# A three-block kernel on one core: the weights' sign by a Prelu, the masks made on chip, the first two tiles in another order

## The chip, the core and the metric

The kernel runs on one core of a Trainium2 chip. A core has a matrix engine (PE, with its weight loads shown apart as PEld), a vector engine (DVE), an engine for activation functions (ACT), GpSimd (POOL) and a queue (SP) that starts the DMA transfers. Each engine takes its own instructions strictly in their order, and waits where an operand or a buffer is not ready. The metric is the time of one execution on the device, in microseconds.

## The reference

Three blocks follow one another on 3072 rows (4 sequences of 768):

```python
la = log_a[:, :, sl]; cum = np.cumsum(la, axis=-1)          # per chunk
L = np.exp(cum[:, :, :, None] - cum[:, :, None, :]) * causal
M = np.einsum('bhin,bhjn->bhij', Cc, Bc) * L
y = M @ xc + (Cc @ state) * exp(cum)                        # attention with a state that is handed on
state = decay_full * state + sum(Bc x xc * decay_from_j)
...
h = y @ w_in;  g = relu(h)**2;  x2 = g @ w_out              # first block: 256 -> 2048 -> 256
a = x2 @ w1;  b = x2 @ w2                                   # second block: 256 -> 1024
out = ((a * b) @ w3) @ w_out2                               # 1024 -> 1024 -> 256
```

All inputs and the result are float32.

## The kernel before, in words

**Products.** Every float32 operand of a product is split into a high part, rounded to the matrix engine's format, and a low part, which is what is left over. A product is three passes (low by high, high by high, high by low). ACT or POOL rounds the high part (`split`, `part_hi`, `conv_parts`), DVE subtracts (`split_lo`, L141).

**Weights.** They come as 44 pieces of 128 x 512 float64 words: 16 of kind "a" (`w_in` and `w_out` of the first block), 4 "o", 16 "3" and 8 "12". SP loads a piece (512 KB), and the kernel makes float32 of it by bit operations on the words: ACT scales the upper words into a float32 (`conv_words`, L196), and for some pieces the lower words too (`ACT_LOW`, L198); otherwise DVE shifts the lower words (L206). Then DVE joins upper and lower words (L207), and a second DVE instruction puts the sign bit in (L210). `conv_parts` then splits the piece (L228 on POOL or L230 on ACT, then L141). Pairs of "3" pieces are multiplied with the "o" pieces on the matrix engine (`w3_product`, L257), so that w3 and the last weight become one.

**Tiles.** The rows are worked off in 6 tiles of 512. A tile has a phase A of 16 steps (`h_mm`, L819: six products of 512 columns; relu on ACT, L833; square on ACT, L841, or DVE, L843; the split; and, a few steps late, `x2_mm`, L866: six more) and a phase B of 8 steps (`a_mm`, `b_mm`, L819 again, and `out_mm`, L919). `SEQ` puts phase A of the second tile straight behind that of the first. In these two phases the pieces are converted, `RATE` pieces a step. `SQ_DVE` names the steps of these two phases whose square DVE takes.

**Attention.** It goes in chunks of 96 rows. Chunks 0 to 5 (units 0 to 2, two chunks each) are worked in `startup`, ahead of all steps; the later ones are placed in slots of the steps (`attention_plan_1` for the chunks of the second tile, `attention_plan` for the rest). The start needs the decays: log(a) by ACT (L343), products with 0/1 masks (L419, L455), which come by DMA as 128 x 904 numbers, exponentials, and from them `e_first`. For a unit, `unit_e1` (L663, L668, then Exp on ACT, L671) spreads the decays, `unit_pad` (L602) and `unit_bi` (L607) prepare C and B, `unit_g0` (L637) multiplies them, `unit_m0` (L679) multiplies both, `chunk_pre` (L578, POOL) scales x, `chunk_ds` (L717) makes the state that `chunk_hand` (L724) hands to the next chunk, and `chunk_y_mm` (L755) makes the result, which `chunk_out` splits into `xt`, the input of the first step.

**What sets the order.** In `startup` and in phase A of the first tile the order on each engine is that of the code (`in_order`, `held`). Behind that a scheduler of the compiler orders the instructions. DMAs keep the order in which the code issues them.

Of the kernel before, what the change touches and what calls it, by code (L numbers as in the profile page):

```python
# [58 lines left out]
def kernel(  # L59
# [969 lines left out]
    def attention_plan_1():  # L1029
        ph = ("A", 0)  # L1030
        for j, s in enumerate(ASLOT):
            g = FIRST[1] + j
            put(ph, s, chunk_pre, g)
            put(ph, s, chunk_mask, g)
            put(ph, s + 1, chunk_g, g, 0)
            put(ph, s + 1, chunk_g, g, 1)
            put(ph, s + 2, chunk_y, g)
        put(ph, 1, unit_bc, 4, BCPLACE)
        put(ph, 1, conv_load, 2)
        for s in range(2):  # L1040
            put(ph, 1 + s, unit_e1, 3, 2 * s, False)
            put(ph, 1 + s, unit_e1, 3, 2 * s + 1, False)
        put(ph, 4, unit_e, 4)
        put(ph, 7, unit_split, 5)
        put(ph, 10, unit_bc, 5)
# [266 lines left out]
```

## Time and profile before

| | us |
|---|---|
| median of three runs | 560.01 |
| lowest, highest | 557.99, 560.12 |
| the profiled execution | 559.61 |
| its span in the profile | 557.9 |

Some 1.7 us of the profiled execution lie outside the span. The profile has, for each engine, the time in which it was busy; the span in stretches; the chain of work that ended last; and groups of like instructions with their mean duration and the idle time of the engine before them. Matrix products are pipelined: a product of 512 columns is shown with some 390 ns, but six of them follow one another in 1.36 us, so a busy matrix engine is not one at its peak. The last three columns of the windows are the clock granted to the matrix engine (as a share of the full one), the DMA share and GB/s.

### The profile page before, as it was taken

How to read it: one execution, taken by the hardware profiler on the slowest of the kernel's cores; microseconds unless marked ns; L12 is line 12 of the kernel's file. 1: busy time of each engine (PE TensorE's matmuls, PEld its weight loads, DVE VectorE, ACT ScalarE, POOL GpSimd, SP SyncE). 2: the span in 40 equal slices, each digit the busy share in tenths (PEclk: the TensorE clock that was granted, in tenths of full speed). 3: DMA queues.
4: the chain of work that ended last, by engine and by line, in shares of the span. 5: the costliest groups of instructions: out<-in, count | busy, mean ns of one | idle time of the engine just before them, and what ended most of it. 6: DMA issues, size and time to landing. Idle time of an engine off the chain costs nothing.

```text
span 557.9 us, 9140 instructions
## 1 busy us (share of the span) xinstructions
PE 544.0 (98%) x3340; PEld 448.5 (80%) x3340; DVE 367.6 (66%) x665; ACT 284.3 (51%) x543; POOL 88.1 (16%) x136
## 2 busy tenths in 40 slices
PE   7979999999999999999999999999999999999997
PEld 5757777889888888888888888888888888888886
DVE  5689999987989575576576556574566474554431
ACT  6699768877875322354333354342435332444332
POOL 7344750000000221004031004020012010000000
PEclk9889999999999999999999999999999999999999
DMA  8697592143454561067250066120173220100001
GB/s 235 231 307 225 176 374 91 39 152 114 164 173 126 135 160 53 0 156 177 68 133 17 16 156 170 24 79 1 36 168 100 57 70 0 39 0 2 0 1 38
DMA packets 56573, 59.46 MB, mean 107 GB/s; under 512 B 33360, under 2 KB 44624, under 8 KB 56528
## 3 DMA queue, kind: packets, MB, share of 16 engines
q1 hardware_dynamic: 56528, 58.88, 36.8%
q8 instruction: 26, 0.43, 0.3%
q14 instruction: 19, 0.16, 0.1%
HBM read 50.20 MB, written 8.65 MB: 105 GB/s over the span
## 4 chain that ended last, share of the span: by engine, by line
PE 81%; DVE 8%; ACT 4%; DMA 4%; issue 1%; SPq 1%; DVEq 0%; ACTq 0%
PE mm L819 43%; PE acc L866 19%; PE acc L919 10%; PE mm L257 4%; PE acc L928 2%; PE y L755 2%; PE g L618 2%; DVE gp L141 2%; DMA xb<-in_xb_dram 1%; DMA raw<-in_raw_dram 1%; DVE cvs L207 1%; DVE wa L141 1%; SPq L93 1%; DVE cvs L210 1%; DMA u<-in_w_dram 1%
## 5 line engine op out<-in xcount | busy, mean ns | idle before, releaser
L819 PE MATMUL mm<-xt,wa 128*128 128x512 f32 x576 | 148.7, 395 | 3.2 <-DVE wa L141 2.0
L849 ACT CAST gp<-tmp 128x512 fp32r<-128x512 f32 x144 | 89.3, 622 | 119.4 <-DVE tmp L907 64.3
L866 PE MATMUL acc<-gp,wa 128*128 128x512 f32 x576 | 146.4, 392 | 1.3 <-DVE gp L141 0.7
L141 DVE TENSOR_TENSOR gp<-tmp,gp 128x512 fp32r<-128x512 f32 x144 | 103.0, 718 | 62.7 <-ACT gp L849 61.9
L819 PE MATMUL mm<-x,w 128*128 128x512 f32 x576 | 143.4, 392 | 0.0
L819 PEld LDWEIGHTS mm<-xt,wa 128*128 128x128 f32 x576 | 107.4, 190 | 26.8 <-ACT tmp L833 2.4
L866 PEld LDWEIGHTS acc<-gp,wa 128*128 128x128 f32 x576 | 106.4, 188 | 24.5 <-DVE gp L141 1.5
L819 PEld LDWEIGHTS mm<-x,w 128*128 128x128 f32 x576 | 105.9, 188 | 21.7 <-ACT tmp L899 0.2
L833 ACT ACTIVATE tmp<-mm 128x512 f32<-128x512 f32 x96 | 57.3, 597 | 50.9 <-PE mm L819 50.2
L919 PE MATMUL acc<-gp,w3o 128*128 128x512 f32 x240 | 63.7, 391 | 0.0
L843 DVE TENSOR_TENSOR tmp<-tmp 128x512 f32<-128x512 f32 x68 | 46.9, 692 | 24.0 <-ACT tmp L833 23.5
L559 POOL TENSOR_SCALAR_AFFINE_SELECT e<-e 96x768 f32<-96x768 f32 x26 | 25.3, 985 | 236.3 <-DMA e<-e_d 228.9
L907 DVE TENSOR_TENSOR tmp<-tmp,mm 128x512 f32<-128x512 f32 x48 | 33.0, 687 | 42.9 <-PE mm L819 42.4
L919 PEld LDWEIGHTS acc<-gp,w3o 128*128 128x128 f32 x240 | 44.8, 188 | 9.4
L899 ACT COPY tmp<-mm 128x512 f32<-128x512 f32 x48 | 28.2, 587 | 41.0 <-PE mm L819 40.7
L578 POOL TENSOR_TENSOR xb<-xb,dec 96x256 f32<-96x256 f32 x32 | 23.1, 723 | 91.9 <-DMA xb<-in_xb_dram 89.2
L624 DVE TENSOR_TENSOR e<-g,e 128x384 f32<-128x384 f32 x52 | 27.6, 551 | 6.5 <-PE g L618 6.0
L257 PE MATMUL mm<-wo,w 128*128 128x256 f32 x128 | 23.7, 284 | 0.4 <-DVE w L141 0.3
L745 DVE SCALAR_TENSOR_TENSOR xb<-xb,through,y 32x64 f32<-32x64 f32 x72 | 20.3, 282 | 3.1 <-PE y L717 1.3
L257 PEld LDWEIGHTS mm<-wo,w 128*128 128x128 f32 x128 | 20.6, 190 | 2.0 <-DVE w L141 1.0
L618 PEld LDWEIGHTS g<-cb,bt 96*128 96x128 f32 x96 | 16.6, 190 | 3.3
L257 PE MATMUL mm<-wo2l,w 128*128 128x256 f32 x64 | 18.1, 283 | 0.0
(111 smaller groups left out, 476.9 us busy)
## 6 DMA issues: line engine op xcount, KB each, us to landing
u<-in_w_dram SPq DMA_DIRECT2D x24, 512.0 KB, 3.9
ua<-in_w_dram SPq DMA_DIRECT2D x16, 512.0 KB, 7.0
e<-e_d SPq DMA_DIRECT2D x40, 192.0 KB, 5.1
xb<-in_xb_dram SPq DMA_DIRECT2D x32, 192.0 KB, 3.8
bt<-hl_d SPq DMA_DIRECT2D x78, 48.0 KB, 2.1
hl_d<-gp SPq DMA_DIRECT2D x9, 384.0 KB, 2.6
cb<-hl_d SPq DMA_DIRECT2D x66, 48.0 KB, 2.0
out_dram<-gp SPq DMA_DIRECT2D x20, 128.0 KB, 3.0
```

What stands on the lines that cost most here:

```text
L141: return nc.vector.tensor_tensor(out=lo, in0=src, in1=hi.bitcast(F32), op=ALU.subtract)
L257: nc.tensor.matmul(acc[:, :DM], v[:, l, e % 4 * P:(e % 4 + 1) * P], wo2[1 + e // 2][r][:, e % 2 * DM:(e % 2 + 1) * DM], start=(n == 0), st ...
L618: nc.tensor.matmul(ps[:, 2 * pp:2 * pp + 2], w, un["c2"][:, pr, :, j * CH:(j + 1) * CH], start=True, stop=True)
L624: nc.vector.tensor_tensor(out=m, in0=ps, in1=m, op=ALU.mult)
L819: i = nc.tensor.matmul(ps, w[m][:, l, col + k * P:col + (k + 1) * P], rhs[k][:, r, :], start=((l, r, k) == (1, 0, 0)), stop=((l, r, k) == ...
L833: nc.scalar.activation(r, ps, AF.Relu)
L843: nc.vector.tensor_tensor(out=g32, in0=r, in1=r, op=ALU.mult)
L849: nc.scalar.copy(g[:, 0, :], d[k])
L866: i = nc.tensor.matmul(acc["x2", t][e], wa[m][:, l, 256 + e * P:256 + (e + 1) * P], g[:, r, :], start=(m == 0 and n == 0), stop=(m == MF - ...
L899: nc.scalar.copy(s, ps)
L907: nc.vector.tensor_tensor(out=p32, in0=prods[t, m], in1=ps, op=ALU.mult)
L919: nc.tensor.matmul(acc["o"][e].rearrange("p s e -> p (s e)"), w3o[m // 2][:, l, m % 2, e * P:(e + 1) * P], g[:, r, :], start=(m == 0 and n ...
```

## The change

The upper words are scaled by a Prelu whose slope for negative numbers is 2^32 times larger, with the sign turned: a negative word comes out positive, with its exponent 32 higher, and the shift by three that joins the words then moves that bit into the sign. The second DVE instruction goes. The masks are no longer loaded whole: 128 x 136 numbers come, and DVE makes the rest (`masks_made`, `masks_inside`, `masks_halves`) with a memset and subtractions. `a` comes without its padding. Which engine rounds a first-block piece's high part, squares and lower words changes (13 of 16 such pieces on POOL as before, but others; `SQ_DVE` 5 and 8 steps instead of none and 4; 12 of the "3" pieces' lower words on ACT instead of 8), and `RATE` of the second tile's phase A goes from 1.55 to 2.1 pieces a step. `startup` and `attention_plan_1` are written in another order; in `startup`, `unit_m0` is now placed one quarter at a time.

```diff
-AHEAD = 6
-ASLOT = (6, 9, 13, 17, 21)
+AHEAD = 5
 LOW_SCALE, LOW_BIAS = 2.0 ** -29 - 2.0 ** -42, 2.0 ** -12 - 0.5
-ACT_LOW = {"a": (0, 1, 2, 3), "o": (), "3": (1, 3), "12": ()}
+ACT_LOW = {"a": (0, 1, 2, 3), "o": (), "3": (0, 2, 3), "12": ()}
...
-SQ_DVE = {0: (), 1: (3, 4, 5, 6)}
+SQ_DVE = {0: (3, 8, 9, 11, 14), 1: (0, 1, 2, 3, 4, 6, 8, 10)}
...
-RATE = {("A", 0): (1, 0), ("A", 1): (1.55, 3), ("B", 0): (1, 0)}
+RATE = {("A", 0): (1, 0), ("A", 1): (2.1, 3), ("B", 0): (1, 0)}
...
         lo_w, hi_w = stage[i][:, :, 0], stage[i][:, :, 1]
-        keep(nc.scalar.activation(v, hi_w.bitcast(F32), AF.Copy, scale=2.0 ** -112))
+        keep(nc.scalar.activation(v, hi_w.bitcast(F32), AF.Prelu, scale=2.0 ** -112, alpha=-2.0 ** 32))
...
         if not act_low(i):
-            nc.vector.tensor_single_scalar(lo_w, lo_w, 29, op=ALU.logical_shift_right)
+            with held():
+                nc.vector.tensor_single_scalar(lo_w, lo_w, 29, op=ALU.logical_shift_right)
         nc.vector.scalar_tensor_tensor(
             out=v, in0=v, scalar=3, in1=lo_w, op0=ALU.logical_shift_left, op1=ALU.bitwise_or
-        )
-        nc.vector.scalar_tensor_tensor(
-            out=v, in0=hi_w, scalar=0x80000000, in1=v, op0=ALU.bitwise_and, op1=ALU.bitwise_or
         )
...
-        if kind == "a" and j > 2:
+        if kind == "a" and j in (0, 1, 3, 4, 6, 7, 8, 9, 10, 11, 12, 13, 15):
             nc.gpsimd.tensor_copy(w[:, 0, :], v)
...
-    m_rel = new_tmp()
-    m_oth = new_tmp()
+    m_all = wts.tile([P, 780], F32, tag="wo0", name="masks")
+    m_rel, m_cum, m_in, m_aft = m_all[:, :512], m_all[:, 512:648], m_all[:, 648:776], m_all[:, 776:]
...
+        nc.vector.memset(warm, 1.0)
+        nc.vector.memset(m_rel, 0.0)
+        nc.scalar.activation(warm, warm, AF.Ln)
...
-        nc.gpsimd.memset(cb.bitcast(F32), 0.0)
...
+        nc.gpsimd.memset(cb.bitcast(F32), 0.0)
...
-    def decays_load(k):
-        if k == 0:
-            dma(out=la, in_=a)
-        elif k == 1:
-            dma(out=m_rel, in_=masks[:, 0:512])
-        else:
-            c = (slice(256, 392), slice(0, 256))[k - 2]
-            dma(out=m_oth[:, c], in_=masks[:, 512 + c.start:512 + c.stop])
+    def decays_load():
+        dma(out=la[:, :192], in_=a[:, :192])
+        dma(out=m_cum, in_=masks[:, 768:904])
+
+    def masks_made():
+
+        nc.vector.tensor_scalar(
+            out=m_aft, in0=m_cum[:, 31:128:32], scalar1=-1.0, scalar2=1.0, op0=ALU.mult, op1=ALU.add
+        )
+        for b in range(4):
+            nc.vector.tensor_scalar(
+                out=m_rel[:, b * P + 32 * b:b * P + P], in0=m_cum[:, 32 * b:P],
+                scalar1=m_cum[:, 32 * b + 31:32 * b + 32], scalar2=None, op0=ALU.subtract
+            )
+
+    def masks_inside():
+
+        c = m_cum[:, :P].rearrange("p (b i) -> p b i", b=4)
+        nc.vector.tensor_tensor(
+            out=m_in.rearrange("p (b i) -> p b i", b=4), in0=c[:, :, 31:32].to_broadcast([P, 4, 32]), in1=c,
+            op=ALU.subtract
+        )
+
+    def masks_halves():
+        nc.vector.tensor_reduce(
+            out=halves, in_=m_cum[:, P:].rearrange("p (q h) -> p h q", h=2), op=ALU.add, axis=mybir.AxisListType.X
+        )
...
+        put(ph, 0, unit_e1, 3, 1, False)
+        put(ph, 0, unit_e1, 3, 3, False)
+        put(ph, 2, unit_e1, 3, 2, False)
+        put(ph, 2, unit_bc, 4, BCPLACE)
+        put(ph, 3, decays_e_out)
+        put(ph, 3, conv_load, 2)
...
-        decays_load(0)
-        decays_load(1)
-        decays_load(2)
-        decays_load(3)
+        decays_load()
+        chunk_xb(0)
+        picks, rounded = constants()
+        picks(0, nc.vector)
         batch_load(0, 0, 1)
-        batch_load(1, 0, 1)
-        chunk_xb(0)
+        picks(1, nc.gpsimd)
         chunk_xb(1)
         batch_load(0, 1, 3)
+        rounded()
+        decays_ln()
+        batch_load(1, 0, 1)
+        masks_made()
+        masks_inside()
+        masks_halves()
+        chunk_xb(2)
+        decays_e_first()
+        decays_cols()
+        unit_e1(0, 1)
...
```

What the new order does on the engines is shown by three places. The first is the DMA queue at the start (`raw` are B and C of the first sequence, the first `raw` of a pair B, `xb` the chunks' x, `ua` first-block pieces). Before:

```order
L93 DMA tmp<-in_a_dram 128x256
L93 DMA tmp<-in_masks_dram 128x512
L93 DMA tmp<-in_masks_dram 128x136
L93 DMA tmp<-in_masks_dram 128x256
L93 DMA raw_111<-in_raw_dram 128x256
L93 DMA raw_113<-in_raw_dram 128x256
L93 DMA xb<-in_xb_dram 96x512 x2
L93 DMA raw_111<-in_raw_dram 128x2x256
L93 DMA raw_113<-in_raw_dram 128x2x256
L93 DMA xb<-in_xb_dram 96x512 x4
L93 DMA ua_129<-in_w_dram 128x1024
```

Now:

```order
L92 DMA tmp<-in_a_dram 128x192
L92 DMA masks<-in_masks_dram 128x136
L92 DMA xb<-in_xb_dram 96x512
L92 DMA raw_153<-in_raw_dram 128x256
L92 DMA xb<-in_xb_dram 96x512
L92 DMA raw_153<-in_raw_dram 128x2x256
L92 DMA raw_170<-in_raw_dram 128x256
L92 DMA xb<-in_xb_dram 96x512
L92 DMA raw_170<-in_raw_dram 128x2x256
L92 DMA ua_245<-in_w_dram 128x1024
L92 DMA raw<-in_raw_dram 128x2x192
```

The two large mask transfers are gone, and three chunks of x stand ahead of the second C transfer (the second `raw` of the later pair) where two did.

The second is the matrix engine in the start, from the second state product (L717 before, L737 now) to the product of B and C for unit 1 (L637 before, L657 now). Before:

```order
L668 MATMUL mm<-e_first,pick 128x192 x2
L717 MATMUL y<-xb,pb 32x64 x4
L755 MATMUL mm<-e,xb 32x96 x8
L663 MATMUL mm<-nmask,ident 128x384
L668 MATMUL mm<-e_first,pick 128x192 x2
L663 MATMUL mm<-nmask,ident 128x384
L668 MATMUL mm<-e_first,pick 128x192 x2
L637 MATMUL g<-cp,bi 128x192 x8
L717 MATMUL y<-xb,pb 32x64 x4
```

Now:

```order
L737 MATMUL y<-xb,pb 32x64 x4
L683 MATMUL mm<-nmask,ident 128x384
L688 MATMUL mm<-e_first,pick 128x192 x2
L683 MATMUL mm<-nmask,ident 128x384
L688 MATMUL mm<-e_first,pick 128x192 x2
L657 MATMUL g<-cp,bi 128x192 x8
```

The result of chunk 0 (L755) stood ahead of unit 1's B and C product; now it stands behind unit 2's (not shown), and two more decay spreads stand between.

The third is DVE around the first step's weights (`cvs` is the joined piece, `wa_...` its split, `gp<-tmp,gp` the split of a step's square, `hl` that of B and C). Before, from the second piece on:

```order
L207 SCALAR_TENSOR_TENSOR cvs<-cvs,ua_133 128x512
L210 SCALAR_TENSOR_TENSOR cvs<-ua_133,cvs 128x512
L141 TENSOR_TENSOR hl<-raw,hl 128x192 x2
L141 TENSOR_TENSOR wa_579<-cvs,wa_579 128x512
L207 SCALAR_TENSOR_TENSOR cvs<-cvs,ua_135 128x512
L210 SCALAR_TENSOR_TENSOR cvs<-ua_135,cvs 128x512
L207 SCALAR_TENSOR_TENSOR cvs<-cvs,ua_399 128x512
L141 TENSOR_TENSOR gp<-tmp,gp 128x512
L210 SCALAR_TENSOR_TENSOR cvs<-ua_399,cvs 128x512
L207 SCALAR_TENSOR_TENSOR cvs<-cvs,ua_506 128x512
L141 TENSOR_TENSOR wa_599<-cvs,wa_599 128x512
L210 SCALAR_TENSOR_TENSOR cvs<-ua_506,cvs 128x512
```

Now, from the same piece's split on:

```order
L140 TENSOR_TENSOR wa_546<-cvs,wa_546 128x512
L140 TENSOR_TENSOR hl<-raw,hl 128x192 x2
L207 SCALAR_TENSOR_TENSOR cvs<-cvs,ua_375 128x512
L140 TENSOR_TENSOR wa_609<-cvs,wa_609 128x512
L207 SCALAR_TENSOR_TENSOR cvs<-cvs,ua_379 128x512
L140 TENSOR_TENSOR wa_662<-cvs,wa_662 128x512
L207 SCALAR_TENSOR_TENSOR cvs<-cvs,ua_377 128x512
L140 TENSOR_TENSOR gp<-tmp,gp 128x512
L207 SCALAR_TENSOR_TENSOR cvs<-cvs,ua_399 128x512
L140 TENSOR_TENSOR wa_617<-cvs,wa_617 128x512
L140 TENSOR_TENSOR wa_688<-cvs,wa_688 128x512
L140 TENSOR_TENSOR gp<-tmp,gp 128x512
```

Each piece has one instruction ahead of its split where it had two, and the first two pieces are split ahead of the first step's squares.

## Rows read from the trace of the kernel before

**Rows 1.** The page, part 1: busy us, share of span, instructions.
```profile
PE 544.0 (98%) x3340; PEld 448.5 (80%) x3340; DVE 367.6 (66%) x665; ACT 284.3 (51%) x543; POOL 88.1 (16%) x136
```

**Rows 2.** Windows: length, then busy PE, PEld, DVE, ACT, POOL, granted clock, DMA.
```profile
0.00:28.00 28.00, 23.68 (x372) 18.31 (x372) 16.92 (x43) 17.80 (x41) 15.35 (x38) 0.94 0.75 234
28.00:45.00 17.00, 13.53 (x53) 10.18 (x53) 15.58 (x23) 16.56 (x36) 8.86 (x11) 0.90 0.86 263
45.00:91.50 46.50, 44.71 (x300) 35.03 (x301) 45.91 (x81) 35.67 (x73) 22.32 (x27) 1.00 0.76 255
91.50:157.00 65.50, 64.48 (x371) 55.91 (x369) 55.71 (x98) 54.93 (x102) 0.00 (x0) 1.00 0.31 105
157.00:228.00 71.00, 71.00 (x429) 58.37 (x428) 51.84 (x102) 29.90 (x59) 11.18 (x17) 1.00 0.45 122
```

**Rows 3.** Timeline of PE, 28 to 95: start, length, instruction, [idle before].
```profile
28.06 1.65 PE L819 MATMUL mm<-xt,wa 128*128 128x512 f32 x6 [0.87 <-ACT xt L144]
...
91.49 3.56 PE L819 MATMUL mm<-xt,wa 128*128 128x512 f32 x15
```

**Rows 4.** Groups of PE, 28 to 91.5: count, busy us, mean ns, idle before.
```profile
L819 PE MATMUL mm<-xt,wa 128*128 128x512 f32 x100 | 28.0, 419 | 3.0 <-DVE wa L141 2.0 <-ACT xt L144 0.9
L866 PE MATMUL acc<-gp,wa 128*128 128x512 f32 x96 | 25.8, 399 | 0.9 <-ACT gp L849 0.6 <-DVE gp L141 0.3
```

**Rows 5.** Chain of waits: start, length, what (whole span).
```profile
5.03 6.23 DMA raw<-in_raw_dram
...
16.02 1.59 PE g L637 x16
...
239.40 2.27 PE acc L866 x10
...
263.50 1.36 PE mm L819 x6
...
322.06 2.27 PE acc L866 x10
```

**Rows 6.** Groups of DVE, 28 to 91.5.
```profile
L141 DVE TENSOR_TENSOR wa<-cvs,wa 128x512 fp32r<-128x512 f32 x15 | 13.7, 912 | 0.6 <-ACT wa L230 0.6
...
L210 DVE SCALAR_TENSOR_TENSOR cvs<-ua,cvs 128x512 uint32<-128x512 uint32 x15 | 11.5, 766 | 0.1
...
L206 DVE TENSOR_SCALAR uo<-uo 128x512 uint32<-128x512 uint32 x4 | 2.3, 574 | 0.0
...
L206 DVE TENSOR_SCALAR u<-u 128x512 uint32<-128x512 uint32 x4 | 1.7, 424 | 0.0
```

**Rows 7.** Groups of ACT, 28 to 91.5.
```profile
L841 ACT ACTIVATE tmp<-tmp 128x512 f32<-128x512 f32 x16 | 10.1, 632 | 0.3
...
L196 ACT ACTIVATE cvs<-ua 128x512 f32<-128x512 f32 x14 | 9.4, 675 | 0.0
```

**Rows 8.** Groups of ACT, 91.5 to 157.
```profile
L230 ACT CAST w<-cv 128x512 fp32r<-128x512 f32 x18 | 11.0, 620 | 2.3 <-DVE cv L210 2.2
...
L198 ACT ACTIVATE u<-u 128x512 uint32<-128x512 uint32 x8 | 5.4, 677 | 0.0
```

**Rows 9.** Groups of DVE, 91.5 to 157.
```profile
L210 DVE SCALAR_TENSOR_TENSOR cv<-u,cv 128x512 uint32<-128x512 uint32 x18 | 12.2, 688 | 0.0
L141 DVE TENSOR_TENSOR w<-cv,w 128x512 fp32r<-128x512 f32 x17 | 11.6, 687 | 0.7 <-ACT w L230 0.7
...
L843 DVE TENSOR_TENSOR tmp<-tmp 128x512 f32<-128x512 f32 x4 | 2.7, 686 | 0.2 <-ACT tmp L833 0.2
```

**Rows 10.** Timeline of DVE, 0 to 20.
```profile
1.05 0.17 DVE L304 MEMSET tmp<- 128x128 f32 x1
2.98 0.29 DVE L342 TENSOR_SCALAR tmp<-tmp 128x256 f32<-128x256 f32 x1 [1.76 <-DMA tmp<-in_a_dram]
...
5.96 0.61 DVE L422 SCALAR_TENSOR_TENSOR e_first<-e_hi,halves,mm 128x384 fp32r<-128x384 f32 x1 [0.42 <-ACT e_hi L421]
...
17.64 1.95 DVE L679 TENSOR_TENSOR e<-g,e 128x384 f32<-128x384 f32 x4 [1.92 <-PE g L637]
```

More of the change, by code (lines that the diff above doesn't have):

```diff
@@ L289 @@
     lp4 = lps[:, 192:320].rearrange("p (v d c) -> p v d c", v=4, d=2)
+    warm = const.tile([P, 1], F32, name="warm")
     def constants():
@@ L1030, in attention_plan_1 @@
         ph = ("A", 0)
[L1031 to L1045, printed above, removed]
-        put(ph, 12, unit_e, 5)
-        put(ph, ASLOT[0] + 3, chunk_xb, 9)
-        put(ph, ASLOT[1] + 3, chunk_xb, 10)
+        put(ph, 0, unit_e1, 3, 1, False)
[4 more added lines that the diff above has]
+        put(ph, 3, conv_load, 2)
+        put(ph, 5, unit_split, 5)
+        put(ph, 5, chunk_mask, 6)
+        put(ph, 6, chunk_g, 6, 0)
+        put(ph, 7, chunk_g, 6, 1)
+        put(ph, 8, chunk_xb, 8)
+        put(ph, 8, chunk_pre, 6)
+        put(ph, 9, chunk_y, 6)
+        put(ph, 9, chunk_xb, 9)
+        put(ph, 9, chunk_xb, 10)
+        put(ph, 9, chunk_mask, 7)
+        put(ph, 9, chunk_g, 7, 0)
+        put(ph, 9, unit_e, 4)
+        put(ph, 10, chunk_g, 7, 1)
+        put(ph, 10, chunk_pre, 7)
+        put(ph, 10, chunk_mask, 8)
+        put(ph, 10, chunk_y, 7)
+        put(ph, 10, chunk_g, 8, 1)
+        put(ph, 12, unit_e, 5)
+        put(ph, 13, unit_bc, 5)
+        put(ph, 13, chunk_mask, 9)
+        put(ph, 13, chunk_mask, 10)
+        put(ph, 15, chunk_pre, 8)
+        put(ph, 15, chunk_xb, 11)
+        put(ph, 15, chunk_g, 8, 0)
+        put(ph, 16, chunk_g, 9, 1)
+        put(ph, 18, chunk_pre, 9)
+        put(ph, 18, chunk_y, 8)
+        put(ph, 18, chunk_g, 9, 0)
+        put(ph, 18, chunk_y, 9)
+        put(ph, 18, chunk_pre, 11)
+        put(ph, 21, chunk_pre, 10)
+        put(ph, 23, chunk_g, 10, 1)
+        put(ph, 28, chunk_g, 10, 0)
+        put(ph, 31, chunk_y, 10)
         put(("B", 0), 8, state_decays)
-        put(ph, 17, chunk_xb, FIRST[2])
-        put(ph, 20, chunk_pre, FIRST[2])
     def startup():
@@ L1103, in startup @@
+        chunk_pre(0)
+        unit_e1(0, 2)
         unit_bi(0, 2)
         unit_pad(0)
-        chunk_pre(0)
-        for q in range(4):
-            unit_e1(0, q)
+        unit_rows(bt)
         unit_g0(0)
+        chunk_pre(1)
+        chunk_xb(4, "w125")
         unit_bi(2, 6)
+        state(0)
         unit_pad(1)
-        chunk_pre(1)
-        state(0)
-        m0(0)
-        chunk_pre(2)
-        unit_e1(1, 0)
-        unit_e1(1, 1)
-        unit_split(3, "w120")
-        state(1)
-        unit_rows(bt)
@@ new lines, in startup @@
+        unit_pad(2)
+        unit_m0(1, 3)
+        unit_m0(1, 0)
+        unit_e1(2, 0)
+        unit_e1(2, 2)
+        conv_load(1)
+        unit_m0(1, 1)
+        unit_m0(1, 2)
+        conv_load(1)
+        conv_load(2)
+        chunk_pre(2)
+        chunk_pre(3)
+        state(2)
+        unit_e1(2, 1)
+        conv_load(1)
+        conv_bits(0)
+        conv_load(1)
+        value(1)
+        chunk_pre(4)
+        unit_g0(2)
+        unit_split(3, "w120")
+        conv_words(1)
+        unit_m0(2, 3)
@@ L1154, in startup @@
-        conv_words(1)
-        value(5)
-        state(5)
         conv_load(1)
         conv_bits(1)
-        unit_split(4, "w121")
-        chunk_xb(8)
-        conv_load(1)
-        owed[6] = lambda: chunk_hand(5, ds[5])
-        conv_words(2)
-        conv_parts(1)
+        unit_m0(2, 2)
+        value(0)
+        state(4)
+        value(2)
+        state(5)
+        chunk_xb(7)
+        conv_words(2)
+        conv_parts(0)
+        value(5)
+        unit_load(5)
+        value(4)
+        conv_parts(1)
@@ L1165, in startup @@
+        owed[6] = lambda: chunk_hand(5, ds[5])
+        decays_e(1)
+        unit_split(4, "w121")
+        unit_bc(3)
         at_piece[0] = 2
```

84 lines of the change are left out of this document (29 added, 55 removed).

## Prediction

> **What bounds the kernel.** I read the page's busy shares first, then the windows. PE is busy in 544.0 of 557.9 us [rows 1], but that hides the start: from 157 us on it is busy without a gap (71.00 of 71.00), from 91.5 to 157 nearly so (64.48 of 65.50), while the first 28 us hold 23.7 us of small products and the stretch from 28 to 91.5 is one in which others set the pace [rows 2]. So the time is: the start up to the first large product (28.06), phase A of the first tile until that of the second begins (91.49, so 63.4 us), and a PE-bound rest [rows 3].
>
> How much of those 63.4 us does PE need? Its groups there are 100 products of L819 and 96 of L866 [rows 4]; six follow one another in 1.36 us [rows 5], so 196 take 44.4 us. The small products of one tile's attention come from the distance between two like points of the chain a tile apart, 239.40 and 322.06 [rows 5]: 82.7 us, of which 16 x 12 and 8 x 18 large products take 76.2 us; 6.5 us are left. PE's need is then about 51, and some 12 us of this phase are waiting. DVE is busy in 15.58 + 45.91 = 61.5 of the 63.5 us, ACT in 16.56 + 35.67 = 52.2, and ACT in 16.56 of the first 17.0 [rows 2]. DVE is the bound, with ACT beside it in the first third. From 91.5 to 157 DVE (55.71) and ACT (54.93) stand at 85% and 84% [rows 2], and PE hardly waits: that is the load which the pipeline bears.
>
> **The start, up to the first large product.** (a) The second C transfer was issued at 5.03 and took 6.23 us, to 11.26 [rows 5]. By the shapes in the order, 1732 KB were queued up to and with it, now 1508 KB; at the 234 GB/s of this stretch [rows 2] that is 1.0 us sooner. (b) The masks put seven DVE instructions and a memset in place of the transfers. None of their shapes is in the trace; the nearest are a memset of 128 columns, 0.17, and a tensor_scalar of 256, 0.29 [rows 10]. Six of the seven then cost 1.0 to 1.7 us ahead of `e_first`, which stood at 5.96 [rows 10]; in exchange three casts and the reduction's wait that stood there go ahead of the log. I take `e_first` as 0.5 later (bounds 0 to 1). (c) Unit 1's product of B and C ran from 16.02 for 1.59 [rows 5] and held DVE, which waited 1.92 and started unit 1's multiplication at 17.64 [rows 10]. On PE it stood behind chunk 0's result, which needs all of unit 0's multiplication. Now it stands ahead of it and waits for C and for unit 0's banks alone. With C 1.0 sooner and PE's detour gone I take unit 1's multiplication as 3.5 us sooner, less the 0.5 of (b): 3. (d) From there to the first large product were 10.4 us (17.64 to 28.06). One sign instruction (0.69 [rows 9]) and one ACT cast of 0.62 [rows 8] go, a third piece's words (two ACT instructions of 0.68 [rows 7, 8]) come in, and the first piece's high part goes to POOL, which is idle by then. ACT limits this part: its busy time of 17.8 us to 28 [rows 2] stays about what it was, and it cannot end before some 21.5. I take 1 us less, from one chain instead of two into the first piece. Sum: first large product 4 us sooner, at 24 (bounds 1.5 and 6.5: ACT without any wait, or nothing but the transfer and half of c).
>
> **Phase A of the first tile.** Off DVE: 15 sign instructions, 11.5 us [rows 6]; of the eight shifts of lower words (2.3 + 1.7 [rows 6]) six move behind this phase, 2.9. Onto it: five squares of 0.69 [rows 9], 3.4. DVE's 61.5 become 50.5. ACT gives up five squares of 0.632 [rows 7], 3.2: 52.2 become 49. The Prelu itself is not in the trace: I price it as the Copy that it replaces, 0.675, and the ACT groups of this size lie between 0.620 and 0.677 [rows 7, 8], so either way 0.06 each, 0.9 us over 15 pieces. Three engines with needs of 51, 50.5 and 49 do not overlap perfectly. At the 85% that the next phase bears, DVE would ask for 59.4; PE alone for 51. The first two pieces are split before the phase begins, where PE before waited for pieces (2.0 of its 3.0 us of visible waits at L819 [rows 4]). I take 57, DVE at 89%: 6.4 us less (bounds 52 and 61, so 11.4 and 2.4 less). In the DMA queue the twelve transfers of unit 3's B and C now stand behind more weights and behind unit 4's, whose split DVE makes after the second piece; if they land late, PE waits ahead of chunk 6's product, and that belongs to the upper bound.
>
> A split of a piece takes 0.912 here and 0.687 from 91.5 on; POOL is busy for 8.86 + 22.32 us here and for 0.00 there [rows 2, 6, 9]. The Trainium skill (SBUF — State Buffer, "SBUF: two separate sides") has DVE and GpSimd share a pair of ports by an exclusive lock, so that the later one stands still for the whole instruction of the other. By that rule POOL, whose work does not shrink, stops DVE as often as before, and the excess of the removed instructions, 15 x (0.766 - 0.688) = 1.2 us, comes back on others: A would be 58.2 and the total 551.9 instead of 550.7. The two durations agree with the rule.
>
> **Phase A of the second tile.** DVE loses 18 sign instructions of 0.688, 12.4, and at 2.1 pieces a step takes five more pieces in this phase (two instructions of 0.69 each, 6.9) and four more squares, 2.7: from 55.7 to 53. ACT takes five more pieces (0.675 + 0.620), four more lower words (0.677), and gives up four squares (0.632): 6.5 + 2.7 - 2.5 = 6.7, and 54.9 become 61.6 of 65.5, 94%. ACT becomes the fuller engine. Between 84%, where PE waits next to nothing, and the 97% of ACT from 28 to 45, where much is lost, I take 1.5 us of new waiting (bounds 0 and 5).
>
> **The rest.** From 157 on PE had no gap, and from the third tile on the order of the large products is the same: five pieces fewer to convert there give 0.
>
> **Sum.** Profiled execution 559.6 (span 557.9 and 1.7 around it; 0.4 below the median of 560.0): -4.0 - 6.4 + 1.5 = 550.7.
>
> **Rivals.** (1) The floor: ACT without waits in the start (-6.5) and phase A held by PE alone at 52 (-11.4), no new wait: 541.7; between, some 543. For it: three balanced needs just below PE's. Against: no stretch of the trace runs with three engines near 97%. (2) Given back: the start gains its 1.5 only, phase A 3, and ACT at 94% costs 3 us in the second tile: 558.1; with the middle values of each, 556. For it: ACT was at 16.56 of 17.0 from 28 to 45, where DVE instructions were not all that PE waited for. Against: DVE's 45.91 of the next 46.5, with ACT at 77% [rows 2]. (3) Slower: the Prelu takes longer than the Copy. ACT's room in the second tile is 65.5 - 61.6 = 3.9 us over about 25 such instructions, 0.16 each; in the first tile 57 - 49 = 8 over 15. Beyond that each 0.1 us costs 2.5 us there. At twice the Copy's time, 0.675 more, it is 12.9 in the second tile and 2.1 in the first: 565.7. From 0.52 more there is no gain left. Against: the ACT groups of this size lie within 0.06. (4) The change could fail to relieve DVE because the new squares take its place; they are 3.4 of 14.4 us removed, so no more than a quarter: in the range.
>
> The Trainium skill (ScalarE: Activation LUTs, "Step-by-step: what each stage is for") gives one element per cycle and lane whatever the function; by it the Prelu costs the Copy's time and the total stays 550.7. No run so far shows it.
>
> **Chances.** My forecast (546 to 555.5) 0.58, the floor 0.16, given back 0.20, slower 0.06. Some 0.5% (2.8 us) is what a measurement of this kernel can tell from no change, so faster means below 557.2: all of the first two and half of "given back", 0.84; the other half 0.10 within; 0.06 slower. The range of 8 in 10 runs from 544.5, within the floor case, to 558, the end of "given back".
>
> **What would show it.** First large product at 24 instead of 28.06; second tile's phase A beginning at 81 instead of 91.49; DVE below 92% between; no L210 and no longer L196 (0.675); ACT above 90% in the second tile's phase A and PE waiting there for relu or rounding; from the third tile on the same 82.7 us a tile. The prediction is wrong if the first large product is not sooner than 26.5, if PE waits for B and C of unit 3, or if the Prelu group is longer than 0.8.

## The result and the profile after

The changed kernel ran in 550.4 us (median of 4 runs), the kernel before beside it in 559.1 us: ratio 0.9838, with a 95% interval of [0.9804, 0.9872]. The forecast was 550.7. Run twice more, it took 549.9 and 550.3 us (0.9843 [0.9824, 0.9862] and 0.9859 [0.9837, 0.9880]). The executions profiled the first and the second time were disturbed (3052 and 1080 us), so the profile below is one of the third time: 550.1 us, span 548.5.

The page, part 1, which answers to [rows 1]:

```profile
PE 539.0 (98%) x3340; PEld 446.5 (81%) x3340; DVE 348.1 (63%) x634; ACT 280.0 (51%) x539; POOL 87.4 (16%) x136
```

The timeline of PE, for [rows 3] (start, length, instruction, idle before):

```profile
25.53 1.58 PE L839 MATMUL mm<-xt,wa 128*128 128x512 f32 x6
...
29.68 1.65 PE L839 MATMUL mm<-xt,wa 128*128 128x512 f32 x6 [2.14 <-ACT tmp L853]
...
82.26 4.27 PE L839 MATMUL mm<-xt,wa 128*128 128x512 f32 x18
```

The first large product comes at 25.53 (28.06 before) and the second tile's phase A at 82.26 (91.49), so phase A of the first tile takes 56.73 us instead of 63.43. (In the kernel before three of the second tile's products ran at 89.43, ahead of its run of 15; now all 18 come together.) The 9.2 us gained by then are nearly the whole gain: the span is 9.4 shorter.

The windows of these stages, for [rows 2] (length, busy PE, PEld, DVE, ACT, POOL, granted clock, DMA share, GB/s):

```profile
25.53:82.26 56.73, 53.80 (x349) 43.37 (x347) 49.18 (x80) 48.37 (x101) 30.67 (x36) 1.00 0.82 260
82.26:148.52 66.26, 66.03 (x379) 57.63 (x378) 49.68 (x86) 56.08 (x107) 0.00 (x0) 1.00 0.39 127
148.52:218.60 70.08, 69.77 (x423) 57.01 (x421) 48.25 (x94) 28.02 (x55) 11.15 (x17) 1.00 0.42 106
```

In phase A DVE is at 87% and ACT at 85%, near the forecast (89% and 86%). In the second tile's phase ACT is at 85% where 94% was forecast. The two later stages together take 136.34 us; before, from 91.49 to the third tile's first large product at 228.13, it was 136.64.

The groups of DVE, then of ACT, from 25.53 to 82.26, for [rows 6, 7]:

```profile
L140 DVE TENSOR_TENSOR gp<-tmp,gp 128x512 fp32r<-128x512 f32 x16 | 14.4, 902 | 1.2 <-ACT gp L869 1.2
L140 DVE TENSOR_TENSOR wa<-cvs,wa 128x512 fp32r<-128x512 f32 x14 | 11.6, 837 | 2.8 <-ACT wa L227 2.1 <-POOL wa L225 0.7
L207 DVE SCALAR_TENSOR_TENSOR cvs<-cvs,ua 128x512 uint32<-128x512 uint32 x14 | 11.0, 785 | 2.0 <-ACT ua L197 1.9
...
L863 DVE TENSOR_TENSOR tmp<-tmp 128x512 f32<-128x512 f32 x5 | 4.0, 806 | 0.0
```

```profile
L195 ACT ACTIVATE cvs<-ua 128x512 f32<-128x512 f32 x13 | 8.8, 679 | 1.5 <-DMA ua<-in_w_dram 1.5
```

L195 is the Prelu: 0.679, where the Copy took 0.675 [rows 7]. The sign instructions (L210) are gone. A split on DVE takes 0.84 to 0.90 us here, where POOL is busy for 30.67 us, against 0.69 in [rows 9], where POOL is idle.

### The profile page after: what moved, and what is told of

It is laid out like the page before. It is cut to its first block, busy times and chain, and to the rows that moved or that the text cites. A ratio compares the mean times of both kernels' runs of the same rounds, so it can differ in the third digit from the quotient of the medians.

```text
span 3050.8 us, 9091 instructions
## 1 busy us (share of the span) xinstructions
PE 3046.3 (100%) x3340; PEld 2172.5 (71%) x3340; DVE 345.7 (11%) x634; ACT 284.2 (9%) x539; POOL 79.2 (3%) x136
## 4 chain that ended last, share of the span: by engine, by line
PE 100%; ACT 0%; issue 0%; DVE 0%; ACTq 0%
PE mm L839 50%; PE acc L886 25%; PE acc L939 10%; PE mm L254 4%; PE acc L948 2%; PE g L638 2%; PE y L775 2%; PE y L737 1%; PE mm L688 1%; PE mm L683 0%; PE mm L775 0%; PE g L657 0%; PE mm L397 0%; PE y L300 0%; PE g L642 0%; PE mm L475 0%
## 5 line engine op out<-in xcount | busy, mean ns | idle before, releaser
L839 PE MATMUL mm<-xt,wa 128*128 128x512 f32 x576 | 795.6, 1695 | 0.0
L886 PE MATMUL acc<-gp,wa 128*128 128x512 f32 x576 | 792.9, 1694 | 0.0
L839 PE MATMUL mm<-x,w 128*128 128x512 f32 x576 | 789.9, 1697 | 0.0
L886 PEld LDWEIGHTS acc<-gp,wa 128*128 128x128 f32 x576 | 518.0, 910 | 223.4 <-issue 217.3
L839 PEld LDWEIGHTS mm<-xt,wa 128*128 128x128 f32 x576 | 517.5, 913 | 218.3 <-issue 215.1
L839 PEld LDWEIGHTS mm<-x,w 128*128 128x128 f32 x576 | 513.0, 910 | 216.5 <-issue 215.3
L939 PE MATMUL acc<-gp,w3o 128*128 128x512 f32 x240 | 337.9, 1691 | 0.0
L939 PEld LDWEIGHTS acc<-gp,w3o 128*128 128x128 f32 x240 | 216.1, 907 | 97.0 <-issue 94.3
L863 DVE TENSOR_TENSOR tmp<-tmp 128x512 f32<-128x512 f32 x77 | 53.0, 689 | 620.2 <-ACT tmp L853 620.2
L254 PEld LDWEIGHTS mm<-wo,w 128*128 128x128 f32 x128 | 104.0, 928 | 7.3 <-issue 6.9
L254 PE MATMUL mm<-wo,w 128*128 128x256 f32 x128 | 108.2, 1032 | 0.0
```

Of the source, the lines that this page charges most:

```text
L254: nc.tensor.matmul(acc[:, :DM], v[:, l, e % 4 * P:(e % 4 + 1) * P], wo2[1 + e // 2][r][:, e % 2 * DM:(e % 2 + 1) * DM], start=(n == 0), st ...
L839: i = nc.tensor.matmul(ps, w[m][:, l, col + k * P:col + (k + 1) * P], rhs[k][:, r, :], start=((l, r, k) == (1, 0, 0)), stop=((l, r, k) == ...
L863: nc.vector.tensor_tensor(out=g32, in0=r, in1=r, op=ALU.mult)
L886: i = nc.tensor.matmul(acc["x2", t][e], wa[m][:, l, 256 + e * P:256 + (e + 1) * P], g[:, r, :], start=(m == 0 and n == 0), stop=(m == MF - ...
L939: nc.tensor.matmul(acc["o"][e].rearrange("p s e -> p (s e)"), w3o[m // 2][:, l, m % 2, e * P:(e + 1) * P], g[:, r, :], start=(m == 0 and n ...
```

## Experiments

All times are medians; each ratio is to the kernel before, run beside it on the same chip, with a 95% interval. "Second tile" means the start of its phase A. In the table at the end P is the Prelu, S the changed start (with the masks), L the second tile's plan, G the settings.

**The changed kernel again.**

> The changed kernel once more, word for word, since its profiled execution was disturbed (3052 us beside 549 to 551 of the others). Theory (start and first tile's phase A): 549 to 551 us; first large product at 23 to 25 us, second tile's phase A beginning at 79 to 83, DVE below 92% busy between, same distance from tile to tile as before (82.7 us). Rival (the gain lies in the start alone): first large product at 19 to 21, phase A of the first tile still 62 to 63 us long.

549.9 us, 0.9843 [0.9824, 0.9862]. The result stands.

**The Prelu alone, in the kernel before.**

```diff
-        keep(nc.scalar.activation(v, hi_w.bitcast(F32), AF.Copy, scale=2.0 ** -112))
+        keep(nc.scalar.activation(v, hi_w.bitcast(F32), AF.Prelu, scale=2.0 ** -112, alpha=-2.0 ** 32))
...
-        nc.vector.scalar_tensor_tensor(
-            out=v, in0=hi_w, scalar=0x80000000, in1=v, op0=ALU.bitwise_and, op1=ALU.bitwise_or
-        )
```

> The kernel before with the Prelu in place of the second bit operation, nothing else. Theory (DVE bounds the first tile's phase A): 44 instructions of 0.69 go from DVE, 15 of them (11.5 us) in that phase; it shortens by 4 to 6 us, total 554 to 556. Rival 1 (the order decides, DVE's load was only cover): 558 to 560. Rival 2 (the Prelu is dearer than the Copy): mean of the scaled words above 0.75 us, total above 560.

558.9 us, 1.0006 [0.9983, 1.0030]: no gain, as the first rival said. Its windows, phase A first and then its end in pieces of 2 us (columns as above):

```profile
25.71:89.22 63.51, 56.79 (x351) 45.08 (x351) 51.91 (x91) 54.85 (x113) 28.16 (x38) 0.96 0.80 261
84.00:86.00 2.00, 0.69 (x20) 0.49 (x20) 1.97 (x5) 1.88 (x4) 0.00 (x0) 1.00 0.01 4
86.00:88.00 2.00, 1.70 (x23) 0.92 (x17) 2.00 (x4) 0.83 (x2) 0.00 (x0) 0.88 0.03 8
88.00:90.00 2.00, 0.82 (x3) 0.68 (x3) 1.66 (x5) 0.42 (x2) 0.00 (x0) 0.50 0.00 0
90.00:92.00 2.00, 2.00 (x7) 1.52 (x6) 0.00 (x0) 0.00 (x0) 0.00 (x0) 0.50 0.00 0
92.00:94.00 2.00, 2.00 (x6) 1.61 (x5) 0.00 (x0) 0.00 (x0) 0.00 (x0) 0.50 0.00 0
```

DVE is down from 61.46 us of the same phase to 51.91, and the phase still takes 63.5. PE comes to a stand at the end, and its timeline says for whom:

```profile
80.02 4.19 PE L863 MATMUL acc<-gp,wa 128*128 128x512 f32 x17
85.51 0.54 PE L752 MATMUL y<-e,xb 128*32 128x96 f32 x16 [1.31 <-DVE e L621]
85.87 0.72 PE L714 MATMUL y<-xb,pb 128*32 128x64 f32 x16
86.90 1.14 PE L816 MATMUL mm<-xt,wa 128*128 128x512 f32 x3 [0.30 <-ACT xt L144]
89.22 6.08 PE L816 MATMUL mm<-xt,wa 128*128 128x512 f32 x15 [1.18 <-ACT xt L144]
```

The first tile's products are done; PE waits for the last chunks of the second tile's attention, whose mask product (L621) stands on DVE behind weight pieces. DVE had itself stood for such a piece just before:

```profile
80.58 0.43 DVE L206 TENSOR_SCALAR u<-u 128x512 uint32<-128x512 uint32 x1 [1.36 <-DMA u<-in_w_dram]
```

After these waits the granted clock is 0.50, the 1.2 GHz level, from 88 to 94: 15 products take 6.08 us, where they took 3.56 in [rows 3]. So the Prelu takes work off DVE, and the order as it stood gives the time back.

**The sign back on DVE, in the changed kernel.**

```diff
-        keep(nc.scalar.activation(v, hi_w.bitcast(F32), AF.Prelu, scale=2.0 ** -112, alpha=-2.0 ** 32))
+        keep(nc.scalar.activation(v, hi_w.bitcast(F32), AF.Copy, scale=2.0 ** -112))
...
+        nc.vector.scalar_tensor_tensor(
+            out=v, in0=hi_w, scalar=0x80000000, in1=v, op0=ALU.bitwise_and, op1=ALU.bitwise_or
+        )
```

> The changed kernel with Copy and the second DVE bit operation put back. Theory: DVE has its 11.5 us again in the first tile's phase A, in an order that leaves less room for it (squares on DVE, 2.1 pieces a step): total 555 to 559, phase A of the first tile 61 to 63 us. Rival (the order alone is the gain): 550 to 552.

574.8 us, 1.0286 [1.0264, 1.0307]. Both expectations fail: the Prelu is worth nothing in the old order and 24.8 us in the changed kernel. The windows of the same stages:

```profile
26.00:90.30 64.30, 54.78 (x342) 41.82 (x341) 56.16 (x89) 46.72 (x98) 29.58 (x36) 1.00 0.74 234
90.30:172.13 81.83, 72.62 (x392) 60.16 (x390) 67.02 (x115) 59.98 (x110) 0.00 (x0) 0.98 0.33 107
```

Against the changed kernel 7.6 us go in the first tile's phase A and 15.6 in the second's. In the second DVE would need 67.0 us, more than the 66.3 that the changed kernel has there.

**The masks alone, in the kernel before.** The functions `decays_load`, `masks_made`, `masks_inside` and `masks_halves` of the change, called in the old start.

> The kernel before with the masks made by DVE, 128 x 136 numbers loaded instead of 128 x 904, and a without padding; order else as before. Theory: transfers 1.0 to 1.4 us sooner, e_first 0.5 to 1 us later, first large product -1 to +0.5 us, total 558 to 560. Rival (the masks' transfer holds the start): first large product 2 us or more sooner, total 557 or less.

559.3 us, 1.0008 [0.9995, 1.0021]: the time as expected. `e_first` comes at 8.18, 2.2 us later than before and not 0.5 to 1.

**The second tile's plan back, in the changed kernel.**

```diff
-AHEAD = 5
+AHEAD = 6
+ASLOT = (6, 9, 13, 17, 21)
...
+        for j, s in enumerate(ASLOT):
+            g = FIRST[1] + j
+            put(ph, s, chunk_pre, g)
+            put(ph, s, chunk_mask, g)
+            put(ph, s + 1, chunk_g, g, 0)
+            put(ph, s + 1, chunk_g, g, 1)
+            put(ph, s + 2, chunk_y, g)
...
```

`AHEAD`, the number of pieces that are loaded ahead, goes back with the plan.

> The changed kernel with the second tile's plan put back to the regular places (a chunk of the attention at product groups 6, 9, 13, 17 and 21, six pieces ahead), the changed start and settings kept. Theory (relief and order need one another: with the old plan the Prelu alone ran ahead up to 82 us and stood from 82 to 94 us for the second tile's last chunks): most of the gain goes, 555 to 558 us. Rival (the changed start alone brings the gain, by its earlier first product and earlier weight loads): 549.5 to 552 us.

554.6 us, 0.9933 [0.9909, 0.9956]: about half of the gain is gone, just short of the theory's range. PE waits at the same place as with the Prelu alone:

```profile
87.29 4.78 PE L840 MATMUL mm<-xt,wa 128*128 128x512 f32 x18 [1.22 <-ACT xt L144]
```

**Prelu and new plan, the rest as before.** The Prelu's edit and the new `attention_plan_1`, without the entries that the old start has done already. `AHEAD` stays at 6.

> The kernel before with the Prelu and the second tile's plan of the change, its start, its loads and its settings as before. Theory: the stall from 82 to 94 us (7 us lost in TensorE's products in the run with the Prelu alone, 2 to 3 in the kernel before) goes, 552 to 555 us. Rival (start alone): 557 to 560 us. Second rival (the weights' transfers, whose queues are full from 60 to 81 us there, set the end of the first tile's phase A in the old start): 556 to 559 us.

562.0 us, 1.0064 [1.0046, 1.0082]: slower than before, which no expectation had. The chain of waits around 50 us (start, length, what):

```profile
47.84 6.41 DMA ua<-in_w_dram
54.25 0.02 issue
54.27 8.92 DMA e<-e_d
...
63.34 0.88 POOL e L556
...
64.25 0.57 DVE e L621
...
64.86 1.09 PE g L619 x4
```

The new plan asks for chunk 6's mask early. Here the load of its decays (`e<-e_d`) stands in SP's queue behind weight pieces and lands at 63.2; PE stands 7.4 us for it (its timeline: idle 7.38 before 64.86). These loads are issued from 51.6 us on, with the Prelu alone from 44.0 and in the changed kernel from 47.0. That is the wait for chunk 6 that the prediction had put into its upper bound, for another transfer.

**The same with the settings.**

```diff
-ACT_LOW = {"a": (0, 1, 2, 3), "o": (), "3": (1, 3), "12": ()}
+ACT_LOW = {"a": (0, 1, 2, 3), "o": (), "3": (0, 2, 3), "12": ()}
...
-SQ_DVE = {0: (), 1: (3, 4, 5, 6)}
+SQ_DVE = {0: (3, 8, 9, 11, 14), 1: (0, 1, 2, 3, 4, 6, 8, 10)}
...
-RATE = {("A", 0): (1, 0), ("A", 1): (1.55, 3), ("B", 0): (1, 0)}
+RATE = {("A", 0): (1, 0), ("A", 1): (2.1, 3), ("B", 0): (1, 0)}
...
-        if kind == "a" and j > 2:
+        if kind == "a" and j in (0, 1, 3, 4, 6, 7, 8, 9, 10, 11, 12, 13, 15):
```

> The run before it with the change's settings as well (squares on VectorE, pace of the second tile's weights 2.1, lower words, upper parts on GpSimd). Theory: 551 to 554 us, within 1.5 us of the run without them. Rival (start alone): 557 to 560 us. If the settings carry the gain, it is over 3 us faster than the run without them.

562.4 us, 1.0078 [1.0049, 1.0107]; the same wait, 3.6 us long. What this run lacks of the change makes the difference of 12.1 us: the start with its masks, but also `AHEAD` at 5 and the `held` around the shift of the lower words. `AHEAD` decides how many pieces stand ahead of such a load, and neither of these two was run by itself. "Start" below means all of this (the plan's price has `AHEAD` in it too).

**The changed kernel, for its profile.**

> The changed kernel word for word, for its profile. Theory and prediction: first large product at 24 us, second tile's phase A at 81 us with no stall of over 3 us between 82 and 95 us, 549 to 551 us. Second rival (transfers): the last weight piece of the first tile lands at least 5 us before the 80.6 us of the run with the Prelu alone.

550.3 us, 0.9859 [0.9837, 0.9880]. The second tile begins at 82.26 and there is no long stall; the second tile is 1.3 us and the first large product 1.5 us later than expected. The transfers fall as a rival: the last two weight pieces of this stretch (of `u`; issue and time to landing added) land at 83.0 and 84.3 us, and with the Prelu alone at 83.1 and 84.4; they are no earlier, and the second tile begins 7 us sooner.

**The Prelu alone with the last chunks earlier.**

```diff
-ASLOT = (6, 9, 13, 17, 21)
+ASLOT = (6, 9, 12, 15, 18)
-        put(ph, 17, chunk_xb, FIRST[2])
-        put(ph, 20, chunk_pre, FIRST[2])
+        put(ph, 15, chunk_xb, FIRST[2])
+        put(ph, 18, chunk_pre, FIRST[2])
```

> The kernel before with the Prelu, and the last chunks of the second tile's attention at product groups 12, 15 and 18 instead of 13, 17 and 21 (the next tile's first chunk two places sooner with them); nothing else. Theory (the Prelu's gain up to 82 us was given back from 82 to 94 us because the last chunk came late, and the products behind it ran at half the clock): 553 to 556.5 us, and no stretch at half the clock after 84 us. Rival (the weight pieces that land at 78 and 80.6 us hold VectorE, wherever the chunk stands): 557 to 560 us.

558.7 us, 1.0008 [0.9992, 1.0024]: the theory in this simple form falls. In the profile (the fastest of its 12 executions, 556.8 us) the clock does stay up, but the wait is still there:

```profile
86.24 0.72 PE L714 MATMUL y<-xb,pb 128*32 128x64 f32 x16
87.27 0.96 PE L816 MATMUL mm<-xt,wa 128*128 128x512 f32 x3 [0.30 <-ACT xt L144]
89.59 3.69 PE L816 MATMUL mm<-xt,wa 128*128 128x512 f32 x15 [1.37 <-ACT xt L144]
```

Moving the last three chunks by one, two and three groups moves the wait by 0.4 us, and to later. The rival's cause is not seen as it was put: DVE does not stand for a weight piece's landing between 60 and 100 us in this profile. But it is busy for 5.93 of the 6 us from 84 to 90, with joins and splits of pieces that are there and the split of the first tile's result. The split of the last chunk's result, which ACT and then PE wait for, comes behind them at 89.08.

**The settings back, in the changed kernel.** The diff of the settings above, reversed.

> The changed kernel with the settings of before: four squares on VectorE, pace 1.55, lower words of pieces 1 and 3, GpSimd's upper parts as before; Prelu, start, plan and masks of the change kept. Theory (settings are a small term, the start, the plan and the Prelu carry the gain together): 550 to 552.5 us. Rival (the settings spend what the Prelu frees, and without them ScalarE bounds the first two tiles): 554 to 558 us.

556.2 us, 0.9958 [0.9942, 0.9974]: 5.9 us more than the changed kernel's third time (on another chip; 5.5 by the two ratios), within the rival's range. Its reason is not seen: ACT is busy for 50.1 of the 61.8 us of phase A. The profiled execution was the slowest of 12 (559.1 us; the fastest took 554.0), so what stands out in it need not be in all. In its windows there are two stalls (columns as above):

```profile
25.86:87.66 61.80, 56.23 (x349) 45.12 (x350) 44.93 (x77) 50.10 (x106) 28.00 (x38) 0.97 0.81 243
...
62.00:64.00 2.00, 0.80 (x4) 0.34 (x2) 0.59 (x1) 1.82 (x5) 0.00 (x0) 1.00 0.76 180
64.00:66.00 2.00, 1.11 (x15) 1.09 (x19) 1.74 (x6) 2.00 (x5) 1.83 (x3) 1.00 0.25 57
66.00:68.00 2.00, 1.56 (x26) 1.33 (x19) 2.00 (x4) 1.97 (x5) 0.19 (x1) 0.82 0.56 164
68.00:70.00 2.00, 2.00 (x6) 1.56 (x5) 2.00 (x4) 1.93 (x5) 0.93 (x1) 0.50 0.74 279
...
102.00:104.00 2.00, 0.04 (x1) 0.04 (x1) 2.00 (x5) 1.86 (x4) 0.00 (x0) 1.00 0.00 0
104.00:106.00 2.00, 2.00 (x12) 2.00 (x13) 1.82 (x4) 1.79 (x4) 0.00 (x0) 0.71 0.01 4
106.00:108.00 2.00, 2.00 (x11) 2.00 (x11) 0.68 (x1) 0.00 (x0) 0.00 (x0) 0.50 0.34 90
```

The waits from 58 to 70 us name the first one's start (us in total, times, longest):

```profile
DVE cvs L207 <- ACT ua L197: 4.3, 1, 4.3
ACT cvs L195 <- DMA ua<-in_w_dram: 3.8, 1, 3.8
```

ACT stands 3.8 us for a weight piece, DVE for ACT, PE for both, and then the clock is at its lower level. The second is PE waiting 2.0 us for a split of DVE (`w`).

**Sign and settings back: start, plan and masks of the change alone.** The two edits together.

> The run before it without the Prelu: sign by VectorE's second operation, settings of before; start, plan and masks of the change. Theory (most of the 24.8 us that the sign's return cost in the changed kernel came from settings that give VectorE more in the second tile's phase A, 81.8 us there against 66.3): 559 to 564 us. Rival (the changed order itself needs VectorE's freed 30 us): 568 to 575 us.

573.7 us, 1.0275 [1.0261, 1.0289]: the rival. The settings are not what makes the changed order slow without the Prelu: it takes as long with either. They do change the Prelu's price, which is 17.5 us without them (556.2 to 573.7) and 24.8 with them. The second tile's phase A takes 77.4 us here and 81.8 in the run before that had the sign back, against 66.3 in the changed kernel; here, at the slower pace of 1.55 pieces a step, the stage behind it loses too (77.5 against 70.1):

```profile
87.31:164.73 77.42, 70.42 (x379) 59.23 (x378) 61.52 (x105) 54.94 (x102) 0.00 (x0) 0.96 0.28 96
164.73:242.22 77.49, 74.31 (x428) 59.15 (x427) 56.19 (x108) 32.38 (x63) 10.50 (x17) 0.98 0.40 108
```

**The masks loaded, in the changed kernel.**

```diff
...
         dma(out=m_cum, in_=masks[:, 768:904])
+        dma(out=m_rel, in_=masks[:, 0:512])
+        dma(out=m_in, in_=masks[:, 512:640])
...
-        for b in range(4):
-            nc.vector.tensor_scalar(
-                out=m_rel[:, b * P + 32 * b:b * P + P], in0=m_cum[:, 32 * b:P],
-                scalar1=m_cum[:, 32 * b + 31:32 * b + 32], scalar2=None, op0=ALU.subtract
-            )
...
```

> The changed kernel with the relative and the inside masks loaded again (0.32 MB, right behind the decays and the cumulative mask) instead of made by VectorE from the cumulative one; all else as changed. Theory (the queues are full up to 24 us in the changed start, so the 0.32 MB cost what they take there, some 1 us at 300 GB/s, and the first large product moves by as much): 550.5 to 552 us. Rival (off the path, as in the kernel before): 549.5 to 550.5 us. Second rival (each part of the change needs all the others): 554 to 558 us.

552.0 us (549.8 to 553.0), 0.9892 [0.9859, 0.9925]. Inconclusive: its interval overlaps that of the changed kernel. In its profile (549.8 us, the fastest of the four) the first large product comes at 24.66, 0.9 us sooner than with the masks made on chip, and the second tile at 82.12, so nothing in the stages of this execution speaks for a loss.

**Together** (the profiled execution's time; in it phase A of the first tile, from its first large product to the second tile's run of 15 or more, and the busy times in it):

| kernel | median | profiled | phase A | DVE | ACT |
|---|---|---|---|---|---|
| before | 557.9 to 559.1 | 559.6 | 63.4 | 61.5 | 52.2 |
| P | 558.9 | 559.0 | 63.5 | 51.9 | 54.9 |
| P, S, G | 554.6 | 556.0 | 61.5 | 49.8 | 47.7 |
| P, S, L | 556.2 | 559.1 | 61.8 | 44.9 | 50.1 |
| P, S, L, G (changed) | 550.3 | 550.1 | 56.7 | 49.2 | 48.4 |
| S, L, G | 574.8 | 573.5 | 64.3 | 56.2 | 46.7 |

Taken out of the changed kernel, the plan costs 4.3 us, the settings 5.9, the start 12.1 and the Prelu 24.8. Put into the kernel before, the Prelu alone and the masks alone are worth nothing. So the parts' prices do not add up to the 8 us of the whole: the Prelu, the start, the plan and the settings work only with one another. For the masks by themselves that is not shown.

## Why the prediction was right, and where its reasons were not

**The sum.** Forecast against the profiled executions: the start -4.0, measured -2.5; phase A -6.4, measured -6.7; the second tile's new waiting +1.5, and no change behind it, measured -0.3 for both together. -8.9 was forecast for the span, -9.4 came. In the medians it is 7.6 to 8.7.

**The start: right in sign, too large, and by luck.** `e_first` was to come 0.5 later; it came 1.8 later, outside the bounds. The second C transfer was to land 1.0 sooner; issued at 5.57, it took 6.2 us and landed at 11.8, 0.5 later than in [rows 5]. Unit 1's multiplication was to come 3 us sooner; it came 2.2 sooner. From there to the first large product 9.4 us were forecast and 10.1 came. The timeline of DVE, for [rows 10]:

```profile
7.78 0.61 DVE L442 SCALAR_TENSOR_TENSOR e_first<-e_hi,halves,mm 128x384 fp32r<-128x384 f32 x1 [1.30 <-ACT e_hi L441]
...
15.40 1.95 DVE L699 TENSOR_TENSOR e<-g,e 128x384 f32<-128x384 f32 x4 [1.22 <-PE g L657]
```

And most of the 2.5 us was not the change's. In the four profiles with the old start and a Prelu, unit 1's multiplication comes at 15.21 to 15.54 and the first large product at 25.63 to 25.96, against 15.40 and 25.53 in the changed kernel. The Prelu is not the reason: in these four its first instruction runs at 17.48 or later, behind that multiplication. The reason is in the profiled execution of before. Its second C transfer landed at 11.26, in those four at 10.2 to 10.6; PE stood 1.46 us ahead of chunk 0's result (0.40 with the Prelu alone), and then the granted clock fell, where it stayed at 1.00 in the others. Its windows (columns as in [rows 2]):

```profile
14.00:16.00 2.00, 2.00 (x24) 1.69 (x13) 1.68 (x4) 0.81 (x2) 1.87 (x4) 0.56 1.02 390
16.00:18.00 2.00, 2.00 (x29) 1.56 (x32) 0.36 (x1) 0.49 (x1) 0.19 (x1) 0.59 1.10 409
```

Unit 1's product of B and C took 1.66 us there. With the Prelu alone, and in the changed kernel, it is:

```profile
14.35 0.93 PE L634 MATMUL g<-cp,bi 32*128 32x192 f32 x16
...
14.40 0.93 PE L657 MATMUL g<-cp,bi 32*128 32x192 f32 x16
```

So the 3 us of step (c) were not there, and the base of the sum was an execution with a late start. By its own length the new start is worth a few tenths. The masks made on chip seem to cost it time: the old start with them has its first large product at 27.50, and the new start with them loaded has unit 1's multiplication at 14.75 and the first large product at 24.66. What the start is worth lies elsewhere: without it the new plan waits for its loads, as the two runs with the old start showed.

**Phase A of the first tile: the size right, the cause not sufficient.** "DVE is the bound" was the step that failed, and that the size came out all the same is in part luck. The Prelu alone took DVE down by 9.6 us, and the phase did not become shorter; with the settings back DVE needs 44.9 us, 4.3 less than in the changed kernel, and the phase is 5.1 longer (in its slowest execution). What holds PE in this phase are single waits in queues that run in order, 1 to 7 us each: for a mask product behind weight pieces on DVE, for a load behind weights in SP's queue, for a piece that ACT stands for. The changed kernel has only one wait of PE over 1 us there, 2.14 at 29.68. That the lower busy times were needed for 57 us to be possible is argued; the runs show that they were not enough without order and settings. The forecast priced them all as relief and so came out right by the whole, not by the part: had it been asked for the Prelu alone, its working would have given some 6 us, and there were none.

**The clock in this phase: a term that the forecast did not have.** Before, PE stood 1.37 us at 37 us, and behind that the granted clock was 0.53 and 0.62 up to 42, which [rows 2] show as 0.90 over 17 us:

```profile
37.85 4.61 PE L819 MATMUL mm<-xt,wa 128*128 128x512 f32 x12
...
38.00:40.00 2.00, 2.00 (x6) 1.53 (x7) 1.59 (x3) 1.97 (x5) 2.00 (x3) 0.53 1.01 386
```

Twelve products take 2.88 us in the changed kernel (at 70.13), whose clock is 1.00 in every 2 us up to 96. Eight of the twelve profiles have such a dip in this phase. But the clock does not make the gain: it stays at 1.00 with the chunks moved and with the sign back too, where the phase takes 64.0 and 64.3 us. And the executions of the kernel before whose mean granted clock was 1.00 (15 of the 64 beside the experiments) took 557.4 to 558.7 us, within what the others took (557.0 to 560.7). The base, at 0.993 and 559.6, lay above them.

**The excess on DVE.** The sign instructions ran 0.078 us each over the 0.688 that they take with POOL idle, 1.2 us for the 15 [rows 6, 9], and the prediction's second figure had this come back on others. It did not. Over 0.688 each, joins, splits and signs spent 9.2 us of this phase before (those of [rows 6] and the two groups below), joins, splits and squares 7.5 now, and 5.9 with the Prelu alone; POOL was busy for 31.2, 30.7 and 28.2 us. Single groups moved both ways: the splits of products rose from 0.787 to 0.902 us, those of weights fell from 0.912 to 0.837 and the joins from 0.891 to 0.785.

```profile
L207 DVE SCALAR_TENSOR_TENSOR cvs<-cvs,ua 128x512 uint32<-128x512 uint32 x15 | 13.4, 891 | 0.3 <-ACT ua L198 0.3
L141 DVE TENSOR_TENSOR gp<-tmp,gp 128x512 fp32r<-128x512 f32 x16 | 12.6, 787 | 0.6 <-ACT gp L849 0.6
```

The Trainium skill (SBUF — State Buffer, "SBUF: two separate sides") has DVE and GpSimd lock each other out for an instruction; the longer durations beside a busy POOL agree with it, but that the excess would stay as a sum is not what the rows show. The phase took 56.7, nearer to the 57 without this term than to the 58.2 with it, but 1.2 us are not to be told apart here.

**The second tile: wrong in mechanism.** Five more pieces were to fall into this phase at pace 2.1; the group of the Prelu on `u` counts 20 there, and that of the Copy counted 20 before. ACT stood at 85%, not 94%, DVE needed 49.7 us and not 53, and PE waited 0.23 us. The 1.5 us did not come.

**The rivals.** The floor did not come: the start took 25.5 us and phase A 56.7, with PE busy for 53.8 of them. The dear Prelu falls: 0.676 (24 pieces of u) and 0.685 (16 of ua) over the whole span, Copy 0.673 and 0.675. "Given back" did not happen in the whole change but is just what the parts do one by one. New squares in place of the relief: the five take 4.0 us of DVE there (L863 above), under half of the 9.6 that the Prelu alone took off it.

**Open.** Why the moved chunks still end at the same time is shown only so far that their last split stands on DVE behind pieces; without these pieces it was not run. Nor is it shown whether the masks on chip are worth something: alone nothing, in the changed kernel between 0 and 2 us. And that the start's worth of 12.1 us lies in the order of its loads is shown only for the wait in the two runs with the old start and the new plan; an order of loads by itself was not run, nor `AHEAD` or `held`.

## What to carry to other kernels

A busy share of 97% does not say that relieving this engine is enough: remove the load alone and see which wait ends last then. Where engines work off queues in order, a cheaper instruction, a start, a plan and a division of work can be one change; each by itself may measure as nothing or as a loss, and should not be rejected for that. And look at the base's own trace beside other executions before a stage of it enters a sum: here 2 us of a stage were that execution's.
